# Own terms of a chunked linear recurrence: a later load of u, another order on GpSimd, and sums one turn later

## The chip, the cores and the metric

The kernel runs on one core of a Trainium2 chip. A core has five engines that each work through their own queue of instructions: TensorE (PE; its weight loads are shown apart as PEld), VectorE (DVE), ScalarE (ACT), GpSimd (POOL) and SyncE (SP, which here issues the loads and stores). The metric is the device time of one execution in microseconds (us), lower is better. The data type is float32 throughout.

## The reference, cut to what matters

The first part is a linear attention with decay: for each of 4 batches and 8 heads a state of 48 x 48 is carried over 768 tokens. The second part is a router with eight experts, one per token, on the rows that the first part gives.

```python
# r, k, v: (B=4, H=8, S=768, D=48);  w, u: (H, D)
for t in range(S):
    kt, vt, rt = (k[:, :, t], v[:, :, t], r[:, :, t])
    cur = np.einsum('bhd,bhe->bhde', u[None] * kt, vt)
    y[:, :, t] = np.einsum('bhd,bhde->bhe', rt, state + cur)
    state = w[None, :, :, None] * state + np.einsum('bhd,bhe->bhde', kt, vt)
# x = y as (B*S, H*D) = (3072, 384); a cosine router picks one of E=8 experts per row
for e in range(E):
    mask = expert_idx == e
    h = np.maximum(x[mask] @ w1[e], 0.0)      # w1[e]: 384 x 1024
    out[mask] = gate_w[mask, None] * (h @ w2[e])
```

The term with `cur` is a token's own term. It is the row `v[t]` times the number `sum_d r[t,d] * u[d] * k[t,d]` of its head. The change concerns where and when this number is worked out.

## The kernel before

The attention is cut into 24 chunks of 128 tokens (6 stretches of the sequence by 4 batches; chunk `i` is stretch `i // 4` of batch `i % 4`). For each chunk TensorE transposes R and the scaled K (`rt`, `kt`), multiplies them to scores (`at`), which DVE masks (`AT`, in two halves), multiplies V by them (`y`, which ACT copies to `yT`), and transposes the result back (`yrows`). DVE adds the own terms `xd` to it and has the rows `X`. The own terms come in three steps: POOL multiplies K by u and by R (`KU`), DVE sums over each head (`diag`), and ACT multiplies V by that sum, head by head (`xd`).

```python
def load(k, i, K=None):                      # AHEAD = 5 chunks ahead
    ...
    nc.sync.dma_start(out=K, in_=of(k.k))
    R = k.Rpad[i % len(k.Rpad)]
    nc.sync.dma_start(out=R[:, :, 0:D], in_=of(k.r))
    V = k.io.tile([128, H, D], F32, name="V", tag="V")
    if i == 0:
        k.u_bc = ...                         # u, repeated on 128 partitions
        nc.sync.dma_start(out=k.u_bc..., in_=...)
    for n in () if i == 0 else (0, 1) if i == 1 else (i,):
        nc.sync.dma_start(out=k.loaded[n][2], in_=of(k.v, n % B))

def scaled(k, i):                            # the K that TensorE reads
    k.nc.gpsimd.tensor_mul(k.Kpad[i % len(k.Kpad)][:, :, 0:D], k.loaded[i][0], k.kpow)

def own_k(k, i):                             # KU: two buffers
    k.KU[i] = k.work.tile([128, H, D], F32, name="KU", tag="KU")
    k.nc.gpsimd.tensor_mul(k.KU[i], k.loaded[i][0], k.u_bc)

def own_r(k, i):
    k.nc.gpsimd.tensor_mul(k.KU[i], k.KU[i], k.loaded[i][1][:, :, 0:D])

def own(k, i):
    own_k(k, i)
    own_r(k, i)

def own_sum(k, i):                           # diag: two buffers
    k.nc.vector.reduce_sum(diag, k.KU.pop(i), axis=AX.X)

def own_rows(k, i, half):                    # xd, four heads at a time
    for h in range(half * H // 2, (half + 1) * H // 2):
        k.nc.scalar.mul(k.xd[i][:, h, :], V[:, h, :], diag[:, h : h + 1])
```

`build_first` loads chunks 0 to 3, works out the powers of the decay, and makes the scores of chunk 0 by another way than the later ones:

```python
    load(k, 0, k.Kpad[0])                    # raw K of chunk 0, scaled in place below
    for i in range(1, AHEAD - 1):
        load(k, i)
    ...
    own_k(k, 0)
    ...                                      # powers wpow, kp, rpow
    kt, rt = turned_k(k, 0), turned_r(k, 0)
    ...                                      # KT[0], RT[0] from kt, rt (DVE)
    nc.scalar.copy(k.kpow..., ps[...])       # kpow, read by scaled
    first = k.Kpad[0]...
    nc.vector.tensor_mul(first, first, ps[:, :, :, 0:D])
```

One turn of the loop, cut to the steps that matter here (`on` runs a step if the chunk exists):

```python
    for i in range(-1, units):               # turn -1, then turns 0 to 23
        ...
        if i >= 0: on(turn_r, i + 1)         # PE rt, DVE RT
        if i == 0: own_sum(k, i)
        if i >= 0: on(turn_k, i + 1)         # PE kt, ACT KT
        if 0 < i < B: own_rows(k, i, 0)      # ACT, first half of xd
        ...
        on(scaled, i + 2)
        if i < 0: own_r(k, 0)
        on(own, i + 2)
        ...
        if 0 <= i < units - 2: on(own_sum, i + 1)
        ...
        on(sums, i)                          # PE y, ACT yT
        on(states, i)                        # PE st
        for n in (0, 1) if i == 0 else (1,) if 0 < i < B else ():
            own_rows(k, i, n)                # ACT, second half of xd
        on(carry, i)                         # DVE state, POOL state
        on(scores, i + 1)                    # PE at
        on(masked, i + 1, 0)                 # DVE AT, first half
        if i == 0: masked(k, i + 1, 1)
        on(rows, i)                          # PE yrows, DVE X
        if i != 0: on(masked, i + 1, 1)      # DVE AT, second half
        ...
        of_group(turn_rows, i - 1)           # PE xp, ACT xT
```

For chunks 4 and 5 POOL makes `xd` in one instruction. The expert part follows after the last chunk; neither it nor the router is touched.

Of the kernel before, what the change touches and what calls it, by code (L numbers as in the profile page):

```python
# [17 lines left out]
B, H, S, D = 4, 8, 768, 48  # L18
# [33 lines left out]
def build_first(k):  # L52


    nc, pool = k.nc, k.aconst
    wc = pool.tile([128, NP], F32, name="wc")
    nc.vector.memset(wc, 1.0)
    with nc.allow_non_contiguous_dma(reason="384 words"):
        for s, q in ((0, nc.sync), (1, nc.scalar)):
            q.dma_start(out=wc[s * DP : s * DP + D, :], in_=k.w.rearrange("(p s) d -> s d p", s=2)[s])  # L60
    k.ones = k.const.tile([128, 128], F32, name="ones")
    nc.vector.memset(k.ones, 1.0)
    wide = k.work.tile([128, 512], F32, name="wide", tag="AT1")
    nc.vector.memset(wide, 1.0)
    k.ident = k.const.tile([128, 128], F32, name="ident")
    make_identity(nc, k.ident)

    for _ in range(WAKE):
        ps = k.ps.tile([128, 512], F32, name="wake", tag="y")
        nc.tensor.matmul(ps, k.ones, wide, start=True, stop=True)  # L70

    k.Kpad, k.Rpad = (
        [pool.tile([128, H, DP], F32, name=f"{name}{i}") for i in range(count)]
        for name, count in (("Kpad", 4), ("Rpad", AHEAD + 2))
    )
    pads = k.Kpad + k.Rpad
    for t in pads:
        nc.gpsimd.memset(t[:, :, D:DP], 0.0)
    load(k, 0, k.Kpad[0])
    for i in range(1, AHEAD - 1):  # L80
        load(k, i)
    load_rows(k)


    nc.gpsimd.tensor_scalar(wc, wc, W_MIN, W_MAX, ALU.max, ALU.min)
    build_numbers(k)
    own_k(k, 0)
    t = pool.tile([128, NP, C], F32, name="wpow")
    half = C // 2
    for p in range(NP):  # L90
        nc.vector.tensor_tensor_scan(
            t[:, p, 0:half], wc[:, p : p + 1].to_broadcast([128, half]), k.ones[:, 0:half], 1.0, ALU.mult, ALU.mult
        )
    nc.vector.tensor_mul(t[:, :, half:C], t[:, :, 0:half], t[:, :, half - 1 : half].to_broadcast([128, NP, half]))
    mid = pool.tile([128, NP], F32, name="mid")
    nc.vector.reciprocal(mid, t[:, :, C // 2])
    kp = k.work.tile([128, NP, C], F32, name="kp", tag="AT0")
    nc.vector.tensor_mul(kp, t[:, :, ::-1], mid[:, :, None].to_broadcast([128, NP, C]))
    k.rpow = pool.tile([128, NP, C], F32, name="rpow")
    for p in range(NP):  # L100
        nc.scalar.mul(k.rpow[:, p, :], t[:, p, :], mid[:, p : p + 1])


    kt, rt = turned_k(k, 0), turned_r(k, 0)
    k.KT[0], k.RT[0] = (k.work.tile([128, NP, C], F32, name=name, tag=name) for name in ("KT", "RT"))
    for p in (slice(0, NP // 2), slice(NP // 2, NP)):
        nc.vector.tensor_mul(k.KT[0][:, p], kt[:, p], kp[:, p])
        nc.vector.tensor_mul(k.RT[0][:, p], rt[:, p], k.rpow[:, p])
    ps = k.ps.tile([128, NP, 2, DP], F32, name="kpT", tag="xp")
    for p in range(NP):  # L110
        nc.tensor.transpose(ps[:, p].rearrange("q s d -> q (s d)"), kp[:, p, :], k.ident)
    k.kpow = pool.tile([128, H, D], F32, name="kpow")
    nc.scalar.copy(k.kpow.rearrange("q (p s) d -> q p s d", s=2), ps[:, :, :, 0:D])
    cast(k)
    first = k.Kpad[0].rearrange("q (p s) d -> q p s d", s=2)[:, :, :, 0:D]
    nc.vector.tensor_mul(first, first, ps[:, :, :, 0:D])
    k.wC = t[:, :, C - 1 : C].to_broadcast([128, NP, D])


# [171 lines left out]
def load(k, i, K=None):  # L291

    nc = k.nc
    c, b = divmod(i, B)

    def of(src, b=b):
        return src[b, :, c * C : (c + 1) * C, :].rearrange("h s d -> s h d")

    K = k.io.tile([128, H, D], F32, name="K", tag="K") if K is None else K[:, :, 0:D]
    nc.sync.dma_start(out=K, in_=of(k.k))  # L300
    R = k.Rpad[i % len(k.Rpad)]
    nc.sync.dma_start(out=R[:, :, 0:D], in_=of(k.r))
    V = k.io.tile([128, H, D], F32, name="V", tag="V")
    k.loaded[i] = (K, R, V)
    if i == 0:
        k.u_bc = k.aconst.tile([128, H, D], F32, name="u_bc")
        nc.sync.dma_start(
            out=k.u_bc.rearrange("p h d -> p (h d)"),
            in_=bass.AP(tensor=k.u.tensor, offset=k.u.offset, ap=[[0, 128], [1, DM]]),
        )  # L310

    for n in () if i == 0 else (0, 1) if i == 1 else (i,):
        nc.sync.dma_start(out=k.loaded[n][2], in_=of(k.v, n % B))
# [16 lines left out]
def own_k(k, i):  # L330
    k.KU[i] = k.work.tile([128, H, D], F32, name="KU", tag="KU")
    k.nc.gpsimd.tensor_mul(k.KU[i], k.loaded[i][0], k.u_bc)  # L332
# [25 lines left out]
def turned_r(k, i):  # L358
    R = k.loaded[i][1]
    rt = k.ps.tile([128, NP, C], F32, name="rt", tag="tp")  # L360
    for p in range(NP):
        k.nc.tensor.transpose(rt[:, p, :], pair(R, p), k.ident)  # L362
    return rt
# [9 lines left out]
def turned_k(k, i):  # L373
    Kw = k.Kpad[i % len(k.Kpad)]
    kt = k.ps.tile([128, NP, C], F32, name="kt", tag="st")
    for p in range(NP):
        k.nc.tensor.transpose(kt[:, p, :], pair(Kw, p), k.ident)  # L377
    return kt
# [476 lines left out]
def attention(k):  # L855
# [17 lines left out]
    for i in range(-1, units):  # L873
        j = i - SETTLED * B
        if 0 < i + AHEAD < units:
            load(k, i + AHEAD)
        whole(logits_out, i - 3)
        if i in ONCE:
            own_rows_once(k, i)
        if i >= 0:  # L880
            on(turn_r, i + 1)
        if i == 0:
            own_sum(k, i)
        if B <= i < units - 1 and i not in ONCE:
            on(own_rows, i, 0)
        if i >= 0:
            on(turn_k, i + 1)
        if 0 < i < B:
            own_rows(k, i, 0)
        whole(turn_logits, i - 3)  # L890
        if i == B + 3:
            norms(k, k.groups[0])
        on(scaled, i + 2)
        if i < 0:
            own_r(k, 0)
        on(own, i + 2)
        for n in SQUARES.get(i, (i - 1,)):
            of_group(squares, n)
        if B <= i < units - 1 and i not in ONCE:
            on(own_rows, i, 1)  # L900
        if i > B + 1:
            whole(norms, i - 2)
        if j == 10:
            k.lists = turned_lists(k, perm, "tp")
            lists = taken_by_rank(k, k.lists)
            first = [Early(k, r, *lists, w) for r, w in zip(LAST, k.weights)]
        whole(choose, i - 3)
        whole(before, i - 3)
        whole(gates, i - 5)
        whole(lanes, i - 5)  # L910
        whole(listed, i - 5)
        if 0 <= i < units - 2:
            on(own_sum, i + 1)
        for step in (ranks, places, located):
            whole(step, i - 4)
        if j == 7:
            load_, count = loads(k, "xp")
        if j == 9:
            expert_of(k, by)
            number = expert_number(k, LAST[0])  # L920
            load_w1(k, number, k.weights[0][0])
        on(sums, i)
        on(states, i)
        for n in (0, 1) if i == 0 else (1,) if 0 < i < B else ():
            own_rows(k, i, n)
        whole(taken, i - 6, "xp")
        whole(exps, i - 4)
        on(carry, i)
        if 0 < i < B + 2:
            next(tables)  # L930
        whole(summed, i - 6)
        if i == B:
            next(emb)
        on(scores, i + 1)
        on(masked, i + 1, 0)
        if i == 0:
            masked(k, i + 1, 1)
        if i == units - 1:
            first[0].turn()
        on(rows, i)  # L940
        if i != 0:
            on(masked, i + 1, 1)
        if i == units - 2:
            own_sum(k, i + 1)
            own_rows_once(k, i + 1)
        of_group(put, i)
        if j == 10:
            load_w2(k, number, k.weights[0][1])
        of_group(turn_rows, i - 1)
        whole(logits, i - 2)  # L950
        if i == 0:
            build_constants(k)
        if i in (1, 2, 3):
            next(emb)
        if B + 2 <= i < B + 2 + len(k.ring):
            k.nc.gpsimd.memset(k.ring[i - B - 2], 0.0)
        if j == 8:
            by = order(k, load_)
        if j == 9:
            settle(k, by, count)  # L960
            perm = turner(k, by)
# [665 lines left out]
```

## Time and profile before

| | before |
|---|---|
| time, median of 3 runs | 397.58 us (396.89 to 397.84) |
| span of the profiled execution | 395.0 us |
| TensorE busy, weight loads busy | 98%, 89% of the span |
| DVE, ACT, POOL busy | 65%, 42%, 41% |
| granted TensorE clock, mean | 0.995 |

The busy shares are averages over stages with different limits. The attention part takes the first 130 us or so, and its turns follow one another at 4.3 us at first (the transposes of the rows begin at 16.34, 20.64 and 24.94 us). In a timeline row the columns are start, duration (both in us), engine, line of the kernel, operation, the tiles written and read, shapes, the number of instructions merged, and in brackets the idle time before the first of them with what ended it.

### The profile page before, as it was taken

The page shows a single profiled execution, that of the slowest core. Times are in us where ns is not written, and L with a number is a line of the kernel's source. Part 1 is how long each engine was busy: PE and PEld are TensorE (multiplying, and loading weights), DVE is VectorE, ACT ScalarE, POOL GpSimd, SP SyncE. Part 2 cuts the span into 40 slices and gives each one's busy share as a digit, 9 for nine tenths or more (in the row PEclk, how much of TensorE's full clock was granted, in tenths as well). Part 3 has the DMA queues.
Part 4 walks back from the last instruction along what each step waited for, and adds up shares of the span by engine and source line. Part 5 has one row for each costly group of instructions (what it writes and reads, how often), then busy time and mean ns, then how long its engine had stood idle before and what let it go on. Part 6 is the DMA issues. An engine that isn't in the chain of part 4 may idle for free.

```text
span 395.0 us, 9252 instructions
## 1 busy us (share of the span) xinstructions
PE 385.5 (98%) x3540; PEld 352.5 (89%) x3540; DVE 255.8 (65%) x603; ACT 167.8 (42%) x500; POOL 163.8 (41%) x219
## 2 busy tenths in 40 slices
PE   7999999999999999999999999999999999999993
PEld 4998989888888777899999999999999999799783
DVE  6897989878888560767667658257275456655601
ACT  4876777777666412332333332233323233133120
POOL 7999896868673242500602402310340250200111
PEclk9999999999999999999999999999999999999998
DMA  8998996777516961245706531424264170150111
GB/s 151 168 218 188 202 203 142 158 156 155 118 42 223 320 235 58 86 163 172 247 14 225 180 125 76 149 97 162 62 222 159 41 239 2 40 181 0 41 39 44
DMA packets 93796, 54.35 MB, mean 138 GB/s; under 512 B 76937, under 2 KB 88380, under 8 KB 93746
## 3 DMA queue, kind: packets, MB, share of 16 engines
q1 hardware_dynamic: 90242, 44.26, 41.8%
q0 software_dynamic: 3296, 9.44, 7.3%
q8 instruction: 29, 0.48, 0.5%
q14 instruction: 21, 0.17, 0.1%
q10 hardware_dynamic: 208, 0.00, 0.0%
HBM read 44.45 MB, written 9.63 MB: 137 GB/s over the span
## 4 chain that ended last, share of the span: by engine, by line
PE 93%; DMA 3%; DVE 1%; SPq 1%; POOL 0%; issue 0%; POOLq 0%; DVEq 0%
PE ps L1235 25%; PE ps L1299 18%; PE at L396 6%; PE y L460 6%; PE ps L1339 5%; PE ps L1353 4%; PE yrows L478 3%; PE early_h L1045 3%; PE early_y L1054 3%; PE y L451 3%; PE rt L362 3%; PE ps L1213 3%; PE ps L1183 2%; PE kt L377 2%; PE st L417 2%; PE xp L564 2%
## 5 line engine op out<-in xcount | busy, mean ns | idle before, releaser
L1099 POOL DMA_INDIRECT out_dram<-y,to x25 | 29.9, 1196 | 173.0 <-DVE Sh L1374 109.2
L1235 PE MATMUL ps<-xTe,w 128*128 128x192 f32 (+3 forms) x336 | 62.9, 327 | 0.0
L1235 PEld LDWEIGHTS ps<-xTe,w 128*128 128x128 f32 x336 | 55.9, 190 | 0.5
L350 ACT ACTIVATE xd<-V,diag 128x48 f32<-128x48 f32 x160 | 40.2, 326 | 0.0
L402 DVE TENSOR_TENSOR AT<-at,umask 128x512 f32<-128x512 f32 x48 | 32.7, 684 | 7.8 <-PE at L396 7.4
L1242 ACT ACTIVATE hT<-hT 128x384 f32<-128x384 f32 (+3 forms) x42 | 22.0, 523 | 32.4 <-DVE hT L1265 19.7
L1299 PE MATMUL ps<-Tw,Sh 128*128 128x192 f32 x192 | 32.5, 326 | 0.0
L1090 POOL DMA_INDIRECT G<-xs,take x25 | 27.7, 1109 | 10.5 <-issue 4.6
L1299 PEld LDWEIGHTS ps<-Tw,Sh 128*128 128x128 f32 x192 | 31.4, 190 | 0.0
L1235 PE MATMUL ps<-Tx,Sw 128*128 128x192 f32 (+3 forms) x168 | 29.7, 326 | 0.0
L1252 DVE TENSOR_TENSOR u<-ps,p 128x384 f32<-128x384 f32 (+3 forms) x14 | 7.8, 558 | 32.0 <-ACT p L1249 17.3
L396 PE MATMUL at<-RT,KT 48*128 48x128 f32 x384 | 28.1, 285 | 0.2
L1235 PEld LDWEIGHTS ps<-Tx,Sw 128*128 128x128 f32 x168 | 27.6, 190 | 0.1
L460 PE MATMUL y<-AT,V 128*48 128x128 f32 (+1 forms) x384 | 26.0, 277 | 0.0
L396 PEld LDWEIGHTS at<-RT,KT 48*128 48x128 f32 x384 | 23.4, 187 | 2.6 <-issue 1.0
L336 POOL TENSOR_TENSOR KU<-KU,Rpad 128x384 f32<-128x384 f32 x24 | 24.1, 1004 | 1.8
L566 ACT COPY xT<-xp 128x384 f32<-128x384 f32 x24 | 11.5, 479 | 28.6 <-PE xp L564 28.6
L460 PEld LDWEIGHTS y<-AT,V 128*48 128x48 f32 (+1 forms) x384 | 19.9, 124 | 4.1 <-issue 3.3
L1299 PE MATMUL ps<-w,hT 128*128 128x192 f32 x128 | 23.4, 326 | 0.0
L332 POOL TENSOR_TENSOR KU<-K,u_bc 128x384 f32<-128x384 f32 x23 | 23.2, 1009 | 0.0
L321 POOL TENSOR_TENSOR Kpad<-K,kpow 128x384 f32<-128x384 f32 x23 | 23.1, 1005 | 0.1
L1262 ACT ACTIVATE hT<-ps 128x384 f32<-128x384 f32 (+3 forms) x14 | 6.9, 490 | 35.7 <-PE ps L1235 35.7
(242 smaller groups left out, 821.6 us busy)
## 6 DMA issues: line engine op xcount, KB each, us to landing
w<-in_moe_w_dram SPq DMA_DIRECT2D x16, 1536.0 KB, 6.7
Rpad<-in_r_dram SPq DMA_DIRECT2D x24, 192.0 KB, 4.1
V<-in_v_dram SPq DMA_DIRECT2D x24, 192.0 KB, 3.9
xs<-X SPq DMA_DIRECT2D x24, 192.0 KB, 2.7
K<-in_k_dram SPq DMA_DIRECT2D x23, 192.0 KB, 3.6
G<-xs,take POOLq DMA_INDIRECT x27, 3.2
out_dram<-y,to POOLq DMA_INDIRECT x25, 3.5
Kpad<-in_k_dram SPq DMA_DIRECT2D x1, 192.0 KB, 3.1
```

Of the source, the lines that this page charges most:

```text
L321: k.nc.gpsimd.tensor_mul(k.Kpad[i % len(k.Kpad)][:, :, 0:D], k.loaded[i][0], k.kpow)
L332: k.nc.gpsimd.tensor_mul(k.KU[i], k.loaded[i][0], k.u_bc)
L336: k.nc.gpsimd.tensor_mul(k.KU[i], k.KU[i], k.loaded[i][1][:, :, 0:D])
L350: k.nc.scalar.mul(k.xd[i][:, h, :], V[:, h, :], diag[:, h : h + 1])
L396: nc.tensor.matmul(at[s][:, p, :], KT[rows, p, :], RT[rows, p, :], start=True, stop=True)
L402: k.nc.vector.tensor_mul(a, k.at[i][s], k.umask[:, None, :].to_broadcast([128, NP, C]))
L460: mm(y[s][u * DP : u * DP + n, q, :], V[:, h * D : h * D + n], AT[s][:, p, :], start=(c == 0 and q == 0), stop=True, skip_group_check=True,)
L1090: nc.gpsimd.indirect_dma_start(out=G[0:n, :], out_offset=None, in_=k.xs[:, :], in_offset=IndirectOffsetOnAxis(ap=take[0:n], axis=0), bound ...
L1099: put = k.nc.gpsimd.indirect_dma_start(out=k.out[:, :], out_offset=IndirectOffsetOnAxis(ap=to, axis=0), in_=y, in_offset=None, bounds_chec ...
L1235: nc.tensor.matmul(ps[:, j, :], weights[:, (f + j) * 128 : (f + j + 1) * 128], moving, start=(first and j == 0), stop=True, skip_group_che ...
L1242: nc.scalar.activation(h, h, ACT.Relu)
L1299: nc.tensor.matmul(ps, a[:, f, :], b[:, f, :], start=(first and f == 0), stop=(f == NF // 2 - 1), skip_group_check=True)
```

## The change

The load of u moves behind the second K and R. The second K is scaled by POOL ahead of the own terms of chunk 0, which so far came between. In the later turns too the scaling goes by one chunk further ahead and stands behind the own terms. The sums over heads (`diag`) of chunks 1 to 3 are taken in the turn that uses them, and no longer in the turn before. The raw K of the first chunk has a tile to itself (the fourth of the `Kpad` ring, which is not needed until chunk 3), so that its own term can be worked out after the scaled K of chunk 0 has been written to the first. The purpose is to let the second chunk's scaled K and R reach TensorE early. The diff, whole but for its line counts:

```diff
-    load(k, 0, k.Kpad[0])
+    load(k, 0, k.Kpad[3])
...
     build_numbers(k)
-    own_k(k, 0)
...
-    kt, rt = turned_k(k, 0), turned_r(k, 0)
+    kt, rt = turned_k(k, 3), turned_r(k, 0)
...
-    first = k.Kpad[0].rearrange("q (p s) d -> q p s d", s=2)[:, :, :, 0:D]
-    nc.vector.tensor_mul(first, first, ps[:, :, :, 0:D])
+    raw, first = (a.rearrange("q (p s) d -> q p s d", s=2)[:, :, :, 0:D] for a in (k.Kpad[3], k.Kpad[0]))
+    nc.vector.tensor_mul(first, raw, ps[:, :, :, 0:D])
...
-    if i == 0:
+    if i == 1:
         k.u_bc = k.aconst.tile([128, H, D], F32, name="u_bc")
...
-        if i == 0:
+        if 0 <= i < B:
             own_sum(k, i)
...
-        on(scaled, i + 2)
         if i < 0:
-            own_r(k, 0)
-        on(own, i + 2)
+            scaled(k, 1)
+            own(k, 0)
+            own_k(k, 1)
+            scaled(k, 2)
+            own_r(k, 1)
+        else:
+            on(own, i + 2)
+            on(scaled, i + 3)
...
-        if 0 <= i < units - 2:
-            on(own_sum, i + 1)
+        if B - 1 <= i < units - 2:
+            own_sum(k, i + 1)
```

## The prediction

> **What bounds the kernel now.** I read first the busy times, then the chain that ended last, then that chain in order of time for the first 30 us (the change touches only the start of the attention part), then the timeline of each engine there. The page:
>
> ```profile
> PE 385.5 (98%) x3540; PEld 352.5 (89%) x3540; DVE 255.8 (65%) x603; ACT 167.8 (42%) x500; POOL 163.8 (41%) x219
> ...
> PE 93%; DMA 3%; DVE 1%; SPq 1%; POOL 0%; issue 0%; POOLq 0%; DVEq 0%
> ```
>
> TensorE is busy almost without a break and makes 93% of the chain. So work taken from POOL, DVE or ACT is worth nothing by itself; only a moment at which TensorE waits counts, and a wait newly given to TensorE is paid in full. The chain in order of time shows where the waiting is:
>
> ```profile
> 2.55 0.68 SPq L307
> 3.23 0.04 issue
> 3.28 0.43 SPq L300
> 3.71 0.04 issue
> 3.75 4.94 DMA Rpad<-in_r_dram
> 8.69 0.14 issue
> 8.82 0.63 PE rt L362 x4
> 9.45 0.44 PE kt L377 x4
> 9.89 1.02 PE y L460 x15
> ```
>
> The chain is a row of loads (L307 is u, L300 is the second K), then the second R, which lands at 8.69 us; from 8.82 us on every following piece is TensorE. Of the early load only that wait is in play. The weight loads show its size, and the next one:
>
> ```profile
> 7.11 1.19 PEld L396 LDWEIGHTS at<-RT,KT 48*128 48x128 f32 x16 [0.39 <-DVE RT L108]
> 8.79 0.42 PEld L362 LDWEIGHTS rt<-ident,Rpad 128*128 128x128 f32 x4 [0.50 <-POOL Kpad L321]
> 9.82 0.85 PEld L460 LDWEIGHTS y<-AT,V 128*64 128x64 f32 x16 [0.17 <-DVE AT L402]
> ```
>
> TensorE's loads end at 8.30 and resume at 8.79. The page names POOL's Kpad, but in the program the transposes of R wait for the load of R and not for Kpad; Kpad (7.67 to 8.67) merely ended at nearly the same time.
>
> Last, ACT, DVE and TensorE in turn 1 (chunk 1 of the 24), where the second half of the change acts:
>
> ```profile
> 14.38 1.01 ACT L350 ACTIVATE xd<-V,diag 128x48 f32<-128x48 f32 x4
> ...
> 14.75 0.54 DVE L341 TENSOR_REDUCE diag<-KU 128x8 f32<-128x384 f32 x1
> ...
> 15.29 0.63 ACT L465 COPY yT<-y 112x256 f32<-112x256 f32 x2
> ...
> 15.80 1.02 ACT L350 ACTIVATE xd<-V,diag 128x48 f32<-128x48 f32 x4
> ...
> 16.34 0.39 PEld L478 LDWEIGHTS yrows<-ident,yT 112*128 112x128 f32 x4
> ```
>
> The diag at 14.75 is that of chunk **2**; chunk 1's was summed a turn before, at 11.71 to 12.26. ACT's queue in a turn is: copy KT, half of xd, copy yT, the other half of xd, copy xT. TensorE needs yT at 16.34 (ready 15.92, 0.42 us to spare), and DVE needs the whole xd for X (17.06 us; ready 16.82).
>
> **What the Trainium skill says.** "PSUM — Partial Sum Buffer", section "Engine vs sequencer instructions", says that the queues of ScalarE, VectorE and GpSimdE are strictly first in, first out. The trace agrees as far as it shows: the yT copy starts at 15.29, though its matmuls ended by 14.88 (13.79 + 1.09 in the timeline of TensorE), behind the xd half issued before it. So a half of xd that waits holds back the yT behind it. "DMA: Bandwidth & Descriptors", section "Queues, rings and completion order", says that each DMA engine takes descriptors in ring order, though completion is not strictly in that order. The trace agrees for these loads: with issue plus time to landing, u lands at 2.55+4.0 = 6.55, the second K at 3.28+4.3 = 7.58, the second R at 8.69. "Perfetto Trace Analysis", section "Optimization Strategy", says to find the gaps of the engine that limits and what each waits for; that is the reading above.
>
> **The change, part by part.**
>
> (a) *u behind the second K and R.* The second R moves from the fifth load to the fourth. u took the stretch between the first R's landing (1.94+3.8 = 5.74) and 6.55, so 0.81 us. The second K should land at 7.58−0.81 = 6.77, the second R at 8.69−0.81 = 7.88. u takes the fifth place and lands at about 8.7. V, needed by the first y, stays sixth.
>
> (b) *Scaling of the second K ahead of KU of chunk 0.* Before: KU 6.68 to 7.68, Kpad 7.67 to 8.67. The scaling needs kpow, which ACT copies at 7.00 to 7.48 from a chain that the change leaves alone. So it runs at about 7.52 to 8.52: 0.15 us earlier, not a full microsecond.
>
> (c) *What that gives TensorE.* The first scores end in the weight loads at 8.30, so rt can begin at 8.33 in place of 8.79, and kt follows at 8.72 with Kpad there since 8.52. That is 0.46 us. The first y would then start at 9.36, if its inputs are there. Its first mask (AT) ends at 8.52 + 0.68 = 9.2. Its V is the sixth load: the spacing of K to R was 8.69−7.58 = 1.11 (1.03 from u to K), so V comes at about 9.75 in both kernels. Then y starts at 9.7 to 9.8 instead of 9.82. I book **0.1 us gained**: the 0.46 is lost again to the next wait. The second mask, done by 9.81, also limits the second half of y.
>
> (d) *Raw first K in its own tile.* One operation still, DVE's 0.56 us; it lets POOL read raw K later. No time.
>
> (e) *POOL's order.* 1.0 us each for Kpad, KU and KU times R, same count. KU of chunk 0 now starts when u lands, 8.7, and its product ends at about 10.75 (before 9.65). The diag of chunk 0 is then 10.8 to 11.35 rather than 10.33 to 10.87. The eight xd multiplies take 1.91 us, to 13.3; X at 13.6 has room. The third Kpad still ends at about 12.7, ahead of its kt (13.15). From turn 0 on Kpad comes a chunk earlier, but TensorE never waited for it after 8.8 us: no gain.
>
> (f) *Sums a turn later for chunks 1 to 3.* This is the cost. The order on the queues: DVE does RT of the next chunk, then diag of chunk i; ACT does xd's first half of chunk i, then yT. In turn 1 diag takes the place that diag of chunk 2 had, less the 0.1 gained: start 14.65, end 15.20. ACT starts the half at 15.24 in place of 14.38. From the rows: half to yT 0.91 start to start, yT 0.63 long, second half starts 0.51 after yT and lasts 1.02. So yT runs 16.15 to 16.78, and yrows, due at 16.24, waits for both halves of yT; TensorE reaches the next piece at about 17.0 instead of 16.6: the **first 0.4 us lost**.
>
> The loss grows, since a loop closes: diag (0.55) → xd, yT, xd (0.91+0.51+1.02 = 2.44) → X, the next DVE start 0.47 later → second AT, 0.60 start to start → RT, 0.60 (18.13 minus 17.53, 14.75 minus 14.15) → next diag. With some 0.09 for two handovers the sum is 0.55+2.44+0.47+0.60+0.60+0.09 = 4.75 us. TensorE's turn is 20.64−16.34 = 4.30. While this loop stands it sets the turn: 0.45 more per turn. The diags start at 14.65, 19.40, 24.15. In turn 3: half at 24.74, yT done at 24.74+0.91+0.63 = 26.28, the last half of yrows loads at 26.35, the next piece (xp) starts at 26.55. Before, xp of that turn began at 25.29. **Lost against before: 1.26 us**, with the 0.1 gain already inside.
>
> In turn 3 the sum of chunk 4 is done as before (the loop is broken; chunks 4 and 5 take xd on POOL), so it grows no more. Nothing after that gives it back, as TensorE is busy for 93.78 of the 94 us from 31 to 125 (busy time by stages). Sum: 397.58 + 1.26 = 398.84, rounded **398.8 us**.
>
> **The rivals.** *First: the start is worth what it seems*, 0.46 us, and the sum a turn later is hidden. For it: V may land before 9.4, and ACT is only 42% busy over the span. Against it: ACT's 42% says nothing about its order, and the margin at yrows is 0.42 us while the half of xd slips by 0.86. It would make 397.1. *Second: the loop is worse than I reckon*, or POOL joins it: the KU product of chunk 4 is due at about 24.2 and diag of chunk 4 must not wait for it; X of chunk 4 needs an xd from POOL, now near 30 instead of 28.2. A slip there adds 0.5 to 1 us: 399.8. *Third: the delay is partly given back* at 129.61 us, where TensorE waits 1.19 us for a gather. The gather hangs on the lists, which hang on the same delayed rows, so I expect at most 0.3 us back: 398.5. A transfer set free by the change cannot help later: loads from then on are issued far ahead.
>
> **Range and chances.** The times of before span 396.89 to 397.84, so ±0.5 is noise. The first rival with noise gives the lower end, the second the upper: 397.3 to 399.9, with 398.8 the middle. 2% is 8 us, and no part can move that: faster 0.01, within 2% 0.98, slower 0.01. On the sign alone I hold slower for four times as likely as faster.
>
> **What would show it.** Right: the second R landed before 8.3 us, and rt near 8.33; the first y near 9.75; ACT idle until about 15.2 before the first half of xd of chunk 1; TensorE's yrows waiting for ACT's yT in turns 1 to 3, some 0.4 to 0.5 us each in all; xp of turn 3 at about 26.5. Wrong: y at 9.36 (V was early; then (c) is too small), or no wait at yrows in turns 1 to 3 (then (f) falls, and 397 is right), or a wait of TensorE on POOL's Kpad or xd.

## The result, and the profile after

The kernel after takes **399.44 us** (median; 399.19 to 400.15) against 397.09 us of the kernel before beside it (396.89 to 397.84). The ratio is 1.0058, with a 95% interval of 1.0045 to 1.0071, so the change costs about 2.3 us. The prediction was 398.8 us, or 1.3 us more. The sign and the mechanism were right, and the size was too small.

The page of the kernel after, busy times and chain of waits:

```profile
PE 386.6 (97%) x3540; PEld 352.3 (89%) x3540; DVE 257.0 (65%) x603; ACT 168.1 (42%) x500; POOL 164.0 (41%) x219
...
PE 85%; DVE 7%; DMA 2%; SPq 2%; ACT 2%; issue 1%; POOL 1%; POOLq 0%; DVEq 0%; ACTq 0%
```

Every engine does the same work as before (same counts, busy times within 1.2 us), but TensorE's share of the chain falls from 93% to 85%, DVE's rises from 1% to 7%, and ACT enters it with 2%. The chain in order of time (start, duration, what) shows where:

```profile
6.55 2.38 SPq L299
...
8.98 4.15 DMA Rpad<-in_r_dram
...
14.28 0.67 DVE RT L369
14.95 0.47 DVE diag L340
15.44 1.01 ACT xd L349 x4
16.45 0.52 ACT yT L464 x2
16.97 0.93 ACT xd L349 x4
17.92 0.56 DVE X L483
18.48 0.60 DVE AT L401
19.08 0.60 DVE RT L369
19.67 0.47 DVE diag L340
```

From 14.95 us on this is the loop of step (f): sum, half of xd, yT, half of xd, X, second mask, RT, next sum. From one sum to the next it takes 19.67 − 14.95 = 4.72 us, and the round after it 4.82. The lines above it are new too: the issue of the third K lasts 2.38 us, so the third R is issued at 8.98 and lands at 13.13. In the kernel before the same two issues are these:

```profile
7.25 0.97 SPq L300 DMA_DIRECT2D K<-in_k_dram  x1
8.26 0.91 SPq L302 DMA_DIRECT2D Rpad<-in_r_dram  x1
```

The weight loads of TensorE in the kernel after (start, duration, what; in brackets the idle time before and what ended it):

```profile
8.54 0.42 PEld L361 LDWEIGHTS rt<-ident,Rpad 128*128 128x128 f32 x4
...
9.90 0.85 PEld L459 LDWEIGHTS y<-AT,V 128*64 128x64 f32 x16 [0.50 <-DVE AT L401]
...
13.17 0.42 PEld L361 LDWEIGHTS rt<-ident,Rpad 128*128 128x128 f32 x4 [0.31 <-DMA Rpad<-in_r_dram]
...
21.53 0.47 PEld L477 LDWEIGHTS yrows<-ident,yT 112*128 112x128 f32 x4 [0.40 <-ACT yT L464]
...
26.49 0.48 PEld L477 LDWEIGHTS yrows<-ident,yT 112*128 112x128 f32 x4 [0.58 <-ACT yT L464]
...
26.92 0.35 PEld L563 LDWEIGHTS xp<-ident,X 128*128 128x128 f32 x3
```

And turn 3 of the kernel before:

```profile
24.94 0.39 PEld L478 LDWEIGHTS yrows<-ident,yT 112*128 112x128 f32 x4
25.29 0.35 PEld L564 LDWEIGHTS xp<-ident,X 128*128 128x128 f32 x3
```

The second R is early enough now: rt has no wait at 8.54. But the first y then waits 0.50 us (for the mask and, by the list of waits, 0.3 us for V), and begins at 9.90, no earlier than before. Then the third R holds TensorE for 0.31, and yT holds it for 0.40 and 0.58 in turns 2 and 3. The piece xp of turn 3 begins at 26.92, against 25.29 before: 1.63 us late.

### The profile page after: what moved, and what is told of

It is laid out like the page before. It is cut to its first block, busy times and chain, and to the rows that moved or that the text cites. A ratio compares the mean times of both kernels' runs of the same rounds, so it can differ in the third digit from the quotient of the medians.

```text
span 397.1 us, 9267 instructions
## 1 busy us (share of the span) xinstructions
PE 386.6 (97%) x3540; PEld 352.3 (89%) x3540; DVE 257.0 (65%) x603; ACT 168.1 (42%) x500; POOL 164.0 (41%) x219
## 4 chain that ended last, share of the span: by engine, by line
PE 85%; DVE 7%; DMA 2%; SPq 2%; ACT 2%; issue 1%; POOL 1%; POOLq 0%; DVEq 0%; ACTq 0%
PE ps L1239 25%; PE ps L1303 18%; PE ps L1343 5%; PE at L395 4%; PE ps L1357 4%; PE y L459 4%; PE early_h L1049 3%; PE early_y L1058 3%; PE ps L1217 3%; PE ps L1187 2%; PE yrows L477 2%; PE y L450 2%; PE rt L361 2%; PE kt L376 2%; DVE AT L401 1%; PE st L416 1%
```

## The experiments

Each experiment is timed against the kernel before on the same chip. On these chips the kernel before took 398.3 to 398.4 us, more than on the first one. To follow where a kernel loses, the table gives the **lateness of TensorE's transposes of the rows** by turn: the start of the first weight load of yrows, minus that start in the first trace of before (12.38, 16.34, ... 129.89 us). A wait that costs something raises the number from one turn to the next. The last column is the whole span minus 395.0 us. Each row is one execution, and executions of one kernel differ: against the median of its kernel the traced one took 1.69 us more in a, 0.77 more in d and 0.67 more in g, 0.77 less in j and 1.83 less in f; in the others it was within 0.35 us.

| kernel | turn 0 | 1 | 3 | 4 | 5 | 6 | 9 | 23 | span |
|---|---|---|---|---|---|---|---|---|---|
| before, once more | 0.71 | 0.91 | 0.91 | 1.13 | 1.13 | 1.13 | 1.13 | 1.16 | 1.3 |
| after | 0.08 | 0.42 | 1.55 | 1.64 | 1.64 | 1.63 | 1.95 | 2.01 | 2.1 |
| after, once more | −0.14 | 0.17 | 1.31 | 1.39 | 1.39 | 2.11 | 2.11 | 2.18 | 2.5 |
| a: only the sums later | 0.69 | 0.99 | 2.12 | 2.21 | 2.20 | 3.64 | 3.64 | 3.64 | 4.7 |
| b: all but the sums | 0.14 | 1.87 | 1.86 | 1.86 | 1.86 | 2.27 | 2.27 | 2.33 | 2.6 |
| d: only POOL's order | 0.74 | 0.84 | 1.11 | 1.11 | 1.69 | 1.69 | 2.27 | 2.31 | 3.4 |
| e: after, u early | 0.79 | 1.12 | 2.25 | 2.34 | 2.33 | 2.33 | 2.65 | 2.95 | 3.1 |
| f: before, u as a row | 0.71 | 0.72 | 0.72 | 0.91 | 0.91 | 0.90 | 0.90 | 1.04 | 1.1 |
| g: xd behind yT | 0.46 | 0.48 | 0.75 | 0.76 | 1.80 | 1.80 | 2.38 | 2.45 | 2.6 |
| i: sums at the end | 0.11 | 0.37 | 0.76 | 0.77 | 1.27 | 1.27 | 1.87 | 2.21 | 2.3 |
| j: i and the old order | −0.14 | −0.04 | −0.04 | −0.03 | 0.92 | 0.92 | 0.92 | 0.92 | 1.0 |
| k: after, the old order | 0.07 | 0.37 | 1.50 | 1.59 | 1.58 | 1.58 | 1.58 | 1.95 | 2.1 |
| l: the best version | −0.26 | −0.16 | −0.14 | −0.14 | −0.14 | −0.14 | 0.06 | 0.05 | 1.1 |

The theory was the loop of step (f), with the early load of R worth little. The rivals were that the order on POOL costs by itself, and that u's new place is what costs.

### a: before, with the sums of chunks 1 to 3 a turn later and nothing else

```diff
-        if i == 0:
+        if 0 <= i < B:
             own_sum(k, i)
...
-        if 0 <= i < units - 2:
-            on(own_sum, i + 1)
+        if B - 1 <= i < units - 2:
+            own_sum(k, i + 1)
```

> The kernel before with one part of the change alone: the sums of chunks 1 to 3 in the turn that uses them. Theory 1 (the loop diag, xd, yT, xd, X, AT, RT, next diag, 4.75 us against TensorE's turn of 4.30, makes nearly all of the loss): diag of chunks 1, 2, 3 near 14.75, 19.5 and 24.3 us, the transposes of the rows of chunk 3 begin near 26.3 instead of 24.94, and the time is 1.2 to 1.5 us over the kernel before, some 0.6 to 0.9 under the changed kernel. Theory 2 (the loss is made by the loads and by POOL's later start): within 0.3 us of the kernel before. Theory 3 (the loss is made by POOL's new order, which meets DVE at other moments): within 0.3 us of before as well.

Measured: 400.07 us against 398.40, ratio 1.0044 (1.0029 to 1.0058). From turn 0 to turn 3 it loses 2.12 − 0.69 = 1.43 us, as the kernel after does (1.55 − 0.08 = 1.47), where the kernel before, once more, loses 0.20. So the loop needs nothing but the late sums.

The trace of a also loses 1.44 us in turn 6, which no theory had. It is the slowest of its six executions (401.76 us), so the median of 400.07 can't hold all of this. VectorE there, in kernel a:

```profile
36.68 2.45 DVE L217 TENSOR_SCALAR tie<-number 128x8 f32<-128x8 f32 x1
```

And GpSimd in the same stretch of kernel a:

```profile
36.66 0.52 POOL L433 TENSOR_TENSOR state<-state,wpow 112x192 f32<-112x192 f32 x1
37.13 1.01 POOL L321 TENSOR_TENSOR Kpad<-K,kpow 128x384 f32<-128x384 f32 x1
38.09 1.02 POOL L332 TENSOR_TENSOR KU<-K,u_bc 128x384 f32<-128x384 f32 x1
39.18 1.00 POOL L336 TENSOR_TENSOR KU<-KU,Rpad 128x384 f32<-128x384 f32 x1
```

A multiplication of 128 x 8 numbers, 0.16 us in the trace of before, lasts 2.45 us. It begins as POOL's `state` has begun, and it ends at 39.13, when POOL has its next gap (39.11 to 39.18). Everything behind it on DVE is late, and TensorE waits 1.63 us for X. "SBUF — State Buffer", section "SBUF: two separate sides", of the Trainium skill says that a pair of SBUF ports is shared under an exclusive lock. It is contended for by GpSimd and by those VectorE operations that run in a mode with two ports, or that have two inputs in SBUF while GpSimd reads SBUF. Whichever starts first has the pair for the whole instruction, and the other blocks. The trace agrees in the timing, but doesn't show in which mode `tie`, with one input, ran. It shows one thing more: here a row of three POOL operations held DVE through all of them.

### b: after, with the sums where they were

```diff
-        if 0 <= i < B:
+        if i == 0:
             own_sum(k, i)
...
-        if B - 1 <= i < units - 2:
-            own_sum(k, i + 1)
+        if 0 <= i < units - 2:
+            on(own_sum, i + 1)
```

> The changed kernel with the sums of chunks 1 to 3 a turn earlier again, as before. Theory 1 in its simple form (take the late sums away and the loss goes): 397.1 to 397.5 us. Against it, by POOL's rows in the changed kernel: the product of chunk 1 ends at 14.1 us (11.7 before), and the sum of chunk 1 now stands ahead of the masks of chunk 1 on DVE. The masks would start near 15.0 instead of 12.6, the second scores near 17.4 instead of 15.66, and the time would be 1.9 to 2.4 us over the kernel before, as slow as the changed kernel. I hold the second for right: then late sums are the price of POOL's late start, and not a free choice.

Measured: 400.06 us against 398.40, ratio 1.0043 (1.0029 to 1.0057). The loop is gone (1.87 in turn 1, 1.86 in turn 3), but turn 1 alone costs 1.87 − 0.14 = 1.73 us. VectorE and then the weight loads in kernel b:

```profile
13.99 0.55 DVE L340 TENSOR_REDUCE diag<-KU 128x8 f32<-128x384 f32 x1 [2.32 <-POOL KU L335]
14.46 0.35 DVE L429 COPY state<-st 112x192 f32<-112x192 f32 x1
```

```profile
14.92 0.42 PEld L376 LDWEIGHTS kt<-ident,Kpad 128*128 128x128 f32 x4 [1.59 <-POOL KU L331]
```

The sum of chunk 1 stands in DVE's queue ahead of the state and the masks, and waits 2.32 us for POOL's product, which ends at 13.95. The state and the masks stand idle behind it. In the program kt is written to the PSUM bank that `st` held, so it can start once DVE's copy of the state ends, at 14.81 (the KU that the row names ends at 14.91 too, but kt doesn't read it). So late sums are not a slip of the change: with u at fifth place and POOL's new start, early sums cost no less in the traces (1.73 us against 1.43 to 1.47 for the loop). The times don't decide it, as b and the kernel after were not timed on the same chip.

### d: before, with POOL's new order and nothing else

```diff
-        on(scaled, i + 2)
         if i < 0:
+            scaled(k, 1)
             own_r(k, 0)
         on(own, i + 2)
+        on(scaled, i + 3)
```

> The kernel before with one part alone: from turn -1 on the scaling stands behind the own terms and one chunk further ahead; loads, the first own term and the sums as before. Theory 1: no wait in turns 1 to 3, so at most the 0.3 to 0.45 us that the changed kernel lost later (in turn 8 to 9, and at turn 21)[...]: 0 to 0.45 us over before. Theory 3 (POOL's order makes the loss): 1.5 us or more over before.

Measured: 399.80 us against 398.40, ratio 1.0029 (1.0017 to 1.0041). Up to turn 3 it loses 0.37 us (the kernel before, once more, 0.20), then 0.58 from turn 4 to turn 5 and 0.58 between turns 6 and 9. For the first of these, the list of waits names DVE's copy of `ent` (0.6 us). That copy is behind the sum of chunk 5, which waited 2.49 us for POOL's xd of chunk 4. For the second it names a wait of kt, 0.4 us, of the kind that is taken up again under i, j and k. The second loss is the same in g and i (0.58 and 0.60), so it is no chance of this one execution. So step (e), "no gain" and no loss, does not hold.

### e: after, with u loaded where it was

```diff
-    if i == 1:
+    if i == 0:
         k.u_bc = ...
```

> The changed kernel with u loaded in its old place. Theory 1: the loop stays, so the transposes of the rows of chunk 3 begin near 26.2 instead of 26.49, as the wait for the third R (0.31 us in turn 0) goes; the time is 0.3 to 0.6 us under the changed kernel. Theory 2 (the loads make the loss): it falls to within 0.5 us of the kernel before.

Measured: 399.97 us against 398.40, ratio 1.0037 (1.0024 to 1.0050). The loop costs the same 1.46 us (turn 0 to turn 3). In turn 0 the kernel is 0.79 late, with TensorE waiting 1.3 us for the second R. So in the traces u's new place is no cost; of the parts of the change that were tried, it is the one that gains. The times don't show it: the ratio of e, 1.0037, is within the interval of the kernel after on another chip (1.0019 to 1.0046, below).

### The kernels before and after once more

No edit; both on the chip of f and g.

> The kernel before once more, for its trace on the same chip as the next runs. In the last group of runs every kernel with u ahead of the second K and R (and so, it seems, the kernel before on that chip, at 398.4 us) began the first transposes of rows at 13.1 us instead of 12.38, as the second R landed near 9.5 us and not at 8.69. If the loads of that chip are simply slower, the second R lands late here too; if it was chance, at about 8.7.

> The changed kernel once more, beside the kernel before on this chip. Theory 1 (the loop of the late sums, 1.47 us by turn 3, and later 0 to 1.5 us by where DVE and POOL meet): 1.0 to 2.4 us over before. Where the second R lands late in the kernel before, the change saves up to 0.6 us of it, and the difference is at the lower end.

Measured: before 398.27 us in a single execution (398.42 in the runs beside it), after 399.57, ratio 1.0032 (1.0019 to 1.0046). The weight loads of before, once more, and then of after, once more:

```profile
9.40 0.42 PEld L362 LDWEIGHTS rt<-ident,Rpad 128*128 128x128 f32 x4 [1.29 <-POOL KU L332]
...
10.53 0.85 PEld L460 LDWEIGHTS y<-AT,V 128*64 128x64 f32 x16 [0.17 <-issue]
```

```profile
8.38 0.42 PEld L361 LDWEIGHTS rt<-ident,Rpad 128*128 128x128 f32 x4
...
9.68 0.85 PEld L459 LDWEIGHTS y<-AT,V 128*64 128x64 f32 x16 [0.44 <-DVE AT L401]
...
16.51 0.47 PEld L477 LDWEIGHTS yrows<-ident,yT 112*128 112x128 f32 x4 [0.41 <-ACT yT L464]
...
21.29 0.47 PEld L477 LDWEIGHTS yrows<-ident,yT 112*128 112x128 f32 x4 [0.40 <-ACT yT L464]
...
26.25 0.47 PEld L477 LDWEIGHTS yrows<-ident,yT 112*128 112x128 f32 x4 [0.59 <-ACT yT L464]
```

Here u's new place gains 10.53 − 9.68 = 0.85 us at the first y, where the first pair gained nothing. In this trace of before the second R, issued at 3.77 as in the first one, is in only at about 9.3 (3.77 + 5.53 in the chain) instead of 8.69. The table says that this is the rule: the four traces with u early on these chips are 0.69 to 0.79 late in turn 0, and the seven with u in fifth place lie between −0.26 and 0.46. The first trace of before is the odd one. That fits the step from 1.0058 to 1.0032, which is about 1 us, and the time of the kernel before, which is 1.2 to 1.3 us less on the first chip.

The last three rows are the loop at work. In the first trace of the kernel after the wait for the third R stood in the place of the first of them. Here the third R is in time, and TensorE waits for yT in each of turns 1 to 3.

### f: before, with u as one row, spread over the partitions by TensorE

```diff
-        nc.sync.dma_start(out=k.u_bc..., in_=...)         # 128 copies of the row
+    nc.scalar.dma_start(out=urow, in_=...)                # one row of 1.5 KB
+    nc.tensor.matmul(ps, k.ones[0:1, :], urow, start=True, stop=True)
+    nc.scalar.copy(k.u_bc..., ps)
```

> The kernel before with u loaded as a single row of 1.5 KB on ACT's queue and spread over the 128 partitions by one multiplication with ones on TensorE, copied out by ACT; POOL's order and the sums as before. The load of 192 KB for u is gone from the queue. By the loads' theory the second R lands 0.8 us earlier and V too, so rt begins near 8.33 and the first y near 9.4: 0.3 to 0.6 us under the kernel before, up to 0.9 where the loads are slow. If V or the masks hold the first y all the same, within 0.2 us of before. Meetings of DVE and POOL may shift it by 0.3 us or more either way.

Measured: 399.69 us against 398.42, ratio 1.0024 (1.0005 to 1.0043), with executions from 397.82 to 402.81; the profiled one, at 397.86, is among the fastest. It takes a load off the queue without touching sums or order. But TensorE's matmul with the row, from 5.44 us on, stands in its queue ahead of the first kt, which begins at 6.47 where the kernel before, once more, begins it at 4.75. Whether the row's landing holds that matmul the trace doesn't say. So the first y is at 10.49, and turn 0 is 0.71 late like the kernel before. Whether a row that lands earlier would help stays open, and the spread of the times isn't explained.

### g: after, with both halves of xd behind yT in turns 1 to 3

```diff
-        if 0 < i < B:
-            own_rows(k, i, 0)
...
-        for n in (0, 1) if i == 0 else (1,) if 0 < i < B else ():
+        for n in (0, 1) if 0 <= i < B else ():
```

> The changed kernel with both halves of xd of chunks 1 to 3 behind the copy of yT in ACT's queue. Theory 1: yT no longer stands behind a half that waits for its sum, so TensorE does not wait for yT at the transposes of rows; X still comes late, after the second half (near 17.8 us for chunk 1). The rows of chunk 3 begin near 25.7 us instead of 26.49, 0.5 to 0.9 us gained on the changed kernel. If the loop closes by X and the masks alone, whatever yT does, nothing is gained.

Measured: 399.10 us against 398.42, ratio 1.0016 (1.0009 to 1.0022), so it loses 0.68 us where the kernel after beside it loses 1.15. This cuts the loop at yT, which no longer waits for a sum. Turn 0 to turn 3 falls from 1.45 us (the kernel after, once more) to 0.29. But from turn 4 to turn 5 1.04 us come back. The weight loads of kernel g:

```profile
32.27 0.31 PEld L563 LDWEIGHTS xp<-ident,X 128*128 128x128 f32 x3 [1.04 <-DVE ent L256]
```

### i, j and k: sums at the end of the turn before, and POOL's old order from turn 3 on

i takes the sums of chunks 1 to 3 out of their new place and puts them at the end of the turn before, behind the masks and ahead of the next RT. j is i with the second edit below as well; k is the kernel after with the second edit alone.

```diff
-        if 0 <= i < B:
+        if i == 0:
             own_sum(k, i)
...
         if i != 0:
             on(masked, i + 1, 1)
+        if 0 <= i < B - 1:
+            own_sum(k, i + 1)
```

```diff
-        else:
+        elif i < 3:
             on(own, i + 2)
             on(scaled, i + 3)
+        else:
+            if i > 3:
+                on(scaled, i + 2)
+            on(own, i + 2)
```

> The changed kernel with the sums of chunks 1 to 3 at the end of the turn before they are used: on DVE behind the masks and rows of that turn and ahead of the next RT (before: ahead of the masks; changed: behind the next RT). POOL's product of chunk 1, done at 14.1 us, is then just in time. Theory 1: ACT's first half of xd no longer waits, so the loop is not closed and the 1.45 us of turns 1 to 3 fall to at most 0.3. The time is 1.0 to 1.5 us under the changed kernel; against the kernel before it is 0.5 us above to 0.8 us below, by how late the second R is on that chip and by the later meetings of DVE and POOL. If the loop was not the cause, it stays as slow as the changed kernel.

> As i_sums_at_end, and from turn 3 on POOL has the order of the kernel before again (scaling ahead of the own terms, turn 3 without a scaling, since that chunk's is done). Theory 3, cut down to the later turns (the new order lets POOL reach its state and xd one instruction later in each turn, and DVE's small instructions then stand until POOL's end): the 0.3 to 0.7 us that the changed kernel loses in turns 4 to 9 go, so 0.3 to 0.7 us under i_sums_at_end, and 0 to 1 us under the kernel before. If those losses are chance, no difference from i_sums_at_end within 0.2 us.

> The changed kernel with only POOL's old order from turn 3 on; the sums stay late. Theory 1: the loop's 1.45 us stays, the later 0.3 to 0.7 us go: 0.3 to 0.7 us under the changed kernel, still 0.3 to 1.5 us over the kernel before. If POOL's order in the later turns costs nothing, it equals the changed kernel.

Measured against 398.31 us: i 399.24, ratio 1.0029 (1.0017 to 1.0041); j 398.71, 1.0011 (1.0003 to 1.0020); k 399.13, 1.0032 (1.0019 to 1.0046).

- Sums at the end of the turn take most of the loop away: turn 0 to turn 3 costs 0.65 in i and 0.10 in j, but 1.43 in k, where they stay late.
- From turn 5 to turn 9 the new order costs 0.60 in i, 0.31 in the first trace of the kernel after and 0.72 in the second. With the old order j and k lose nothing there. In the medians j is 0.53 below i, but the intervals of the two ratios still touch. And k's ratio is no better than that of the kernel after once more, and k loses 0.37 of it again by turn 23, by a wait whose cause stays open. So what the order costs rests on the traces more than on the times.

What the order does is seen in the kernel after, in turn 7. VectorE:

```profile
45.91 0.95 DVE L674 TENSOR_SCALAR tile<-pos 128x4 int32<-128x4 int32 x1
...
46.84 0.97 DVE L650 TENSOR_SCALAR ssq<-ssq 128x4 f32<-128x4 f32 x1
```

and GpSimd at the same time:

```profile
45.83 1.00 POOL L335 TENSOR_TENSOR KU<-KU,Rpad 128x384 f32<-128x384 f32 x1
46.79 1.00 POOL L320 TENSOR_TENSOR Kpad<-K,kpow 128x384 f32<-128x384 f32 x1
```

Each of DVE's tiny operations lasts until a POOL operation has ended. In the trace of before the same two take 0.58 and 0.16 us. There ssq begins at 44.75, in the gap that POOL leaves between KU and its product (44.74 to 44.82). These two cost TensorE nothing (1.64 us late in turn 7, 1.63 in turn 8). The one that does is `sum`, an addition to 128 x 4 numbers a turn later; here are `sum`, the state behind it, and TensorE's wait:

```profile
50.90 0.64 DVE L660 TENSOR_SCALAR sum<-sum 128x4 f32<-128x4 f32 x1
...
53.61 0.34 DVE L431 TENSOR_TENSOR state<-state,st 112x192 f32<-112x192 f32 x1
```

```profile
54.07 0.42 PEld L376 LDWEIGHTS kt<-ident,Kpad 128*128 128x128 f32 x4 [0.34 <-POOL what L706]
```

POOL's product runs from 50.51 to 51.51, and `sum` lasts until it has ended (51.54). The state is late by that, and kt takes the PSUM bank that the state leaves at 53.95, as in b; `what`, which the row names, ended at 54.06 beside it. In k `sum` begins at 50.27, as POOL's gap begins (50.28 to 50.35), and takes 0.17 us, and kt has no wait. In the seven traces with the new order throughout `sum` takes 0.63 to 0.65 us, and in five of them (the first of the kernel after, d, e, g and i) kt waits 0.33 to 0.45.

The order on POOL changes nothing in the sum of its work, but it changes which of DVE's small operations meet which of POOL's long ones. The old order has such meetings too: in the first trace of before `mask` (128 x 8) lasts 1.65 us at 24.25, where it takes 0.22 in the kernel after. No wait of TensorE follows there.

Kernel j also shows what lay beneath the loop. VectorE in turn 4, and TensorE's weight load that waits for it:

```profile
29.29 0.55 DVE L340 TENSOR_REDUCE diag<-KU 128x8 f32<-128x384 f32 x1 [1.53 <-POOL xd L354]
...
30.02 1.22 DVE L211 SCALAR_TENSOR_TENSOR turned<-qt,own,turned 128x64 f32<-128x64 f32 x1
31.17 0.17 DVE L256 COPY ent<-ps 128x24 f32<-128x24 f32 x1
```

```profile
31.39 0.31 PEld L563 LDWEIGHTS xp<-ident,X 128*128 128x128 f32 x3 [0.95 <-DVE ent L256]
```

In j POOL's xd of chunk 4 starts at 28.42, 1.04 us later than before (27.38). The sum behind it is as late (29.29 against 28.25), then `turned` is held for 1.22 us, and TensorE waits 0.95 us for `ent`. In the kernel after POOL's xd is later still (29.77), but TensorE doesn't notice, for the loop has by then made it 1.6 us late itself. So part of the loop's price would have been paid anyway.

### l: j, with `ent` copied by ACT and two steps of tables later

```diff
-    nc.vector.tensor_copy(k.ent[:, :, 0:E], ps)
+    nc.scalar.copy(k.ent[:, :, 0:E], ps)
...
-        if 0 < i < B + 2:
+        if 0 < i < B or i in (9, 13):
             next(tables)
```

> As j_end_and_old_order, with the one wait that was left there taken away: the copy of the experts' embeddings (ent) out of PSUM goes to ACT, which is idle then, and DVE's two small steps of the tables that stood in turns 4 and 5 move to turns 9 and 13. In j the transposes of rows in turn 4 waited 0.95 us for DVE's copy, which stood behind a sum that POOL, about 1 us behind since the start, released late. If POOL's lost microsecond reaches TensorE only there, the wait goes, chunk 5 begins its rows near 34.9 to 35.1 us, and the time is 0.7 to 0.95 us under j and 0.3 to 0.8 us under the kernel before. If POOL's lateness merely comes back in another wait (masks or the scaled K a turn later), it is within 0.3 us of j.

Measured: 397.92 us against 398.32, ratio 0.9987 (0.9979 to 0.9995). It is the only version that beats the kernel before, by 0.4 us of the medians. From turn 1 to turn 6 it loses 0.02 us, and after the last turn it is 1.11 us ahead of the kernel before, once more. But the expert part loses about 1.0 us of it (0.05 late in turn 23, 1.1 at the end). TensorE waits there 0.6 us for ACT's `earlyh`; a and d show the same wait and the same loss. What holds that ACT operation stays open; the trace names only `remote`. The kernel before with these last two edits alone was not tried, so how much of the gain is due to the change proper is open.

## Why the prediction was right or wrong

- **(a), (b), (c), the early part: mechanism right, size off.** rt had no wait, and began at 8.54 rather than 8.33. The scaling of (b) ran from 7.69 to 8.68, no earlier than before, and held nothing up. The rest was lost to the next wait (mask and V), as booked, and the first y came at 9.90 (9.7 to 9.8 predicted). The gain of 0.1 us came out as −0.08 in the first pair. There I had not seen that the third K's issue would last 2.38 us, so that the third R, issued at 8.98 instead of 8.26, would hold TensorE for 0.31. On another chip the same step is worth 0.85. The prediction took the landing times from a single trace, which is the odd one of the five with u early, though it suits the shorter times of before on that first chip.
- **(d)** nothing was seen that speaks against it; it was not tried by itself.
- **(f), the loop: right.** Predicted 4.75 us a round, measured 4.72 and 4.82. The cost from turn 0 to turn 3 is 1.43 to 1.47 us in all five traces with late sums and the first half of xd ahead of yT (after, after once more, a, e, k), wherever u and POOL's order stand. Where the third R was late (0.31 us in the first trace of after, 0.15 in a, 0.17 in e), its wait took the place of as much of the first wait for yT, and the sum stayed. So the 0.4 us forecast for turn 1 are seen as such only in after once more and in k. At xp of turn 3 I had 26.55, and it was 26.92. The 0.37 us are 0.22 in the start of the first sum (14.87 for 14.65), 0.05 in the two rounds, and 0.10 from the last sum to xp.
- **(e) and "it grows no more": wrong.** After turn 3 the kernel after loses 0.46 more by turn 23 (1.55 to 2.01), of which 0.32 are lost between turns 7 and 9, and after once more it loses 0.72 in turn 6 alone. I had counted POOL's operations and asked whether TensorE waits for Kpad. I had not asked which of DVE's operations run beside them.
- **The rivals.** The first, that the sums are hidden, falls: yT ended the wait in turns 2 and 3, and in after once more in turn 1 too. The second, that POOL's xd and the sum of chunk 4 or 5 join in, is real (0.95 in j, 1.04 in g) but lies hidden behind the loop in the kernel after. The third, that some comes back at the gather, did not happen: 2.01 late in turn 23, 2.1 at the end.
- **The sum.** Of the measured 2.35 us, the loop gives about 1.47, the rest up to xp of turn 3 0.16 (1.63 in all), and what comes after it about 0.4; the spans of the two profiles differ by 2.1. The last 0.2 to 0.3 us between this pair of traces and the medians are not assigned. On the other chip the medians differ by 1.15 us, close to the 1.26 of the prediction, but that is luck: there the early part gained 0.85 at the first y instead of 0.1, so that only 0.40 of the loss was left by turn 3 (1.31 − 0.91), and turn 6 then added 0.72.

## What to carry to other kernels

When an operation moves in an in-order queue, follow the circle that it closes over all engines, and compare its sum with the turn of the bounding engine: 4.75 against 4.30 us was readable beforehand, to 0.1 us. An engine off the path is not harmless because it is 41% busy. POOL's start, a microsecond later (7.69 us for 6.68), left early sums that block DVE and late sums that close a loop; the end of the turn, tried in i and j, was the better place. And a change of POOL's order moved small operations of DVE into its way. Before a load is moved for a gain of half a microsecond, take the landing times from more than one execution, for here they differ by more than that.

## What the runs showed of the hardware

- DVE's small operations from SBUF to SBUF are stretched while POOL multiplies: `tie` (128 x 8) from 0.16 to 1.02 us in the kernel after once more and to 2.45 in a, `ssq` (128 x 4) from 0.16 to 0.97, `sum` (128 x 4) from 0.17 in k to 0.64 in the kernel after, `turned` (128 x 64) from 0.28 in the kernel after to 1.22 in j. Operations that read PSUM kept their time beside POOL (AT 0.68 us, X 0.54 to 0.56), and so did the sum over KU (0.54 us for 128 x 384).
- The issue of a load on SyncE is not a fixed cost. The third K's took 2.38 us in the kernel after and 0.97 in the first trace of before, with the same loads ahead of it in another order; there the issues of the two V ahead of it took 2.69 together, and 4.07 in the second trace. The first four loads of K, R and u took 0.43 to 0.7.
- The early loads differ from one chip or execution to the next by more than the 0.46 us that the change could gain at rt: the second R, issued at 3.75 and 3.77 us, took 4.94 and 5.53 us to land in two traces of the same kernel.
